# Gated linear recurrence feeding an ELU feed-forward block: the recurrence in 64-token chunks on four 64 by 64 array tiles, instead of 128-token chunks on two

## The chip, the cores and the metric

The kernel runs on one core of a Trainium2 chip. The metric is the device time of one execution in microseconds; lower is better. The engines are named as in the profile: PE is TensorE's matrix multiplication and PEld its loading of stationary weights, DVE is VectorE, ACT ScalarE, POOL GpSimd, SP the engine that issues most DMA transfers. L12 is line 12 of the kernel before.

## The reference

Two blocks follow each other. The first is a recurrence for each of 4 batches and 8 heads over 768 tokens, with a state of 48 by 48 and a gate for each of its rows:

```
f = sigmoid(f_logit)
for t in range(768):
    state = f[t][:, None] * state + outer(k[t], v[t])
    y[t]  = q[t] @ state
```

The second takes the outputs of all heads of a token side by side (3072 tokens by 384), multiplies by w_in (384 by 2048), applies ELU, which is h where h is positive and exp(h) − 1 elsewhere, and multiplies by w_out (2048 by 384). The inputs q, k, v and f_logit are float32; the weights come as 64-bit floats and are converted on the chip.

## The kernel before

`fast` (L356) does the work; `general` (L17) is a slower form for inputs outside its range, which a flag selects at the end. The tokens are cut into 12 units of 256 (U), three to a batch. Each unit has two chunks of 128 tokens (C). Heads lie in pairs: of each pair one head is on partitions 0 to 47 and the other on 64 to 111 (`HALF`); `FULL` names the two halves of 64 partitions.

For one unit, `gates` and `decays` (L522, L535) turn the gate into running products: ScalarE makes 1 + exp(−f) in place, VectorE scans it into g, takes the reciprocal p, and multiplies q by p, while POOL multiplies k by g. The scan starts anew at each chunk: POOL copies every C-th column into `restart` and sets it to zero in f. After that the recurrence inside a chunk is plain matrix work on TensorE, and between chunks one state is passed on:

- `transposed` (L562): k of one chunk, four head pairs, is transposed on TensorE into PSUM (psT) and copied by ScalarE to kn.
- `scores` (L570): for each head k times q of one chunk (psS, one PSUM bank for each half of the partitions), then VectorE multiplies by the causal mask into at.
- `advance` (L587): kn times v (psU); VectorE adds the state and multiplies by the chunk's decay, giving the next state. A batch's last chunk has no successor and skips this and its transpose.
- `outputs` (L608): v times at, and state times q, summed in psY; a batch's first chunk has no state and skips the second part. ScalarE copies psY to xt. After the second chunk, six DMA transfers issued by SP move the rows of the fourth head pair into the unused rows 48 to 63 and 112 to 127 of the first three (16 rows each, `PAD`), so that xt has three full blocks of 128 rows.

The feed-forward block goes in 16 steps per unit. `up` (L689) multiplies a block of w_in with xt (psH, 128 by 256, two buffers), ScalarE and VectorE apply ELU into gg; `down` (L705), two steps later (HLAG), multiplies gg with w_out and sums in psM.

The order of TensorE's work is written out by hand. In the main loop (L765 to L791), while unit m goes through the 16 steps of the feed-forward block, the attention of unit m + 1 is done in between: `attention` (L673) says behind which step each piece stands, and step s takes the pieces of entry s − 5. So before, steps 5 to 14 hold transposes, scores, update, scores, transposes, outputs, update, outputs. `prepare` (L553) issues one head pair's decays in each of the first steps. The start-up (L414 to L788, until `start.close()`) runs in the written order; later, a scheduler of the framework orders each engine's queue, and in the trace TensorE's order is the written one while VectorE does work of later units (decays, and the check of the weights' range at L504) early, as its inputs arrive. Unit 0 has a form of its own, `outputs_direct` (L638).

A product of float32 shows as two matmuls and two weight loads in the profile, a transpose as one. Where a matmul uses at most 64 rows or columns of the array, it occupies a tile of it: scores use two tiles of 64 rows by 128 columns, updates and the v part of outputs two of 128 by 64, the state part of outputs two of the four tiles of 64 by 64.

Of the kernel before, what the change touches and what calls it, by code (L numbers as in the profile page):

```python
# [8 lines left out]
FP32 = mybir.dt.float32  # L9
# [346 lines left out]
def fast(ctx: ExitStack, tc: tile.TileContext, q, k, v, f_logit, w_in, w_out, out, flag):  # L356
# [37 lines left out]
    vts, gts, pts, ats, kns, xts, sts = {}, {}, {}, {}, {}, {}, {}  # L394

    def load(u, other=None):

        b, s0 = u // UPB, (u % UPB) * U
        for n in "fkq":
            for r in range(2):  # L400
                ((other or nc.sync) if r else nc.sync).dma_start(
                    out=qkf[u % NB][n][HALF[r]],
                    in_=src[n][b, r::2, :, s0 : s0 + U].rearrange("p d s -> d p s"),
                )
        vts[u] = sb.tile([128, NCU, DM], FP32, tag="v", name=f"v{u}", bufs=3)
        nc.sync.dma_start(out=vts[u][:], in_=v[b, s0 : s0 + U].rearrange("(c t) n -> t c n", t=C))

    def blank(i, *engines):
# [13 lines left out]
    causal = cst.tile([128, C], FP32, name="causal")  # L422
# [3 lines left out]
        pattern=[[1, C]], channel_multiplier=-1,  # L426
    )
    for i in range(1, NB):
        blank(i, nc.gpsimd)
    fine = cst.tile([128, HP, NCU], FP32, name="fine")  # L430
    nc.vector.memset(fine[:], 1.0)
    py = ps.tile([128, HP, C], FP32, tag="y", name="psY")
# [89 lines left out]
    def gates(u, by_chunk=False):  # L522
# [4 lines left out]
        for i in range(2):  # L527
            a = f[:, :, i * C : (i + 1) * C] if by_chunk else f[:, 2 * i : 2 * i + 2]
            nc.scalar.activation(a, a, AF.Exp, scale=-1.0)
            nc.scalar.activation(a, a, AF.Copy, bias=1.0)  # L530
            if not by_chunk:
# [3 lines left out]
    def decays(u, pairs, cols):  # L535
        t = qkf[u % NB]
        g, p_ = gts[u], pts[u]
        for p in range(pairs.start, pairs.stop):
            a = t["f"][:, p, cols]
            nc.vector.tensor_tensor_scan(  # L540
                out=g[:, p, cols], data0=a, data1=a if cols.stop - cols.start == C else restart[:, p, cols],
# [20 lines left out]
    def transposed(u, c, bank="t"):  # L562

        pt = ps.tile([128, HP, 128], FP32, tag=bank, name=f"psT{u}_{c}")
        for p in range(HP):
            nc.tensor.transpose(pt[:, p, :], in_=qkf[u % NB]["k"][:, p, c * C : (c + 1) * C], identity=ident[:])  # L566
        kns[u, c] = sb.tile([128, HP, 128], FP32, tag="kn", name=f"kn{u}_{c}")
        nc.scalar.copy(kns[u, c][:], pt[:])  # L568

    def scores(u, c):  # L570
        t = qkf[u % NB]
        cols = slice(c * C, (c + 1) * C)
        at = ats[u, c] = sb.tile([128, 2, HP, C], FP32, tag="at", name=f"at{u}_{c}")
        pc = [ps.tile([128, HP, C], FP32, tag=f"s{r}", name=f"psS{u}_{c}_{r}") for r in range(2)]
# [6 lines left out]
        for r in range(2):  # L581
            nc.vector.tensor_tensor(  # L582
                out=at[:, r], in0=pc[r][:], in1=causal[:].unsqueeze(1).broadcast_to([128, HP, C]),
# [3 lines left out]
    def advance(u, c):  # L587

        if u % UPB == UPB - 1 and c == NCU - 1:
            return  # L590
        pu = ps.tile([128, HP, D], FP32, tag="t", name=f"psU{u}_{c}")
        for p in range(HP):
            for r in range(2):
                h = 2 * p + r
                nc.tensor.matmul(  # L595
                    pu[FULL[r], p], lhsT=kns[u, c][:, p, FULL[r]], rhs=vts[u][:, c, h * D : (h + 1) * D],
                    start=(p == 0), stop=(p == HP - 1), skip_group_check=True,
                )
        s = sb.tile([128, HP, D], FP32, tag="state", name=f"state{u}_{c}", bufs=3)
        now = pu[:]  # L600
        if u % UPB or c:
            nc.vector.tensor_tensor(out=s[:], in0=pu[:], in1=sts[u, c][:], op=ALU.add)
            now = s[:]
        decay = pts[u][:, :, (c + 1) * C - 1 : (c + 1) * C].broadcast_to([128, HP, D])
        nc.vector.tensor_tensor(out=s[:], in0=now, in1=decay, op=ALU.mult)
        sts[(u, c + 1) if c < NCU - 1 else (u + 1, 0)] = s

    def outputs(u, c):  # L608
        t = qkf[u % NB]
        cols = slice(c * C, (c + 1) * C)  # L610
        first = u % UPB == 0 and c == 0
        if c == 0:
            xts[u] = sb.tile([128, HP, U], FP32, tag="xt", name=f"xt{u}", bufs=3)
        at = ats.pop((u, c))
        for p in range(HP):
            for r in range(2):
                h = 2 * p + r
                nc.tensor.matmul(  # L618
                    py[HALF[r], p, :], lhsT=vts[u][:, c, h * D : (h + 1) * D], rhs=at[:, r, p],
                    start=(p == 0), stop=first, skip_group_check=True,  # L620
                )
        if not first:
            s = sts[u, c]
            for p in range(HP):
                for r in range(2):
                    nc.tensor.matmul(  # L626
                        py[HALF[r], p, :], lhsT=s[HALF[r], p], rhs=t["q"][HALF[r], p, cols],
                        start=False, stop=True, skip_group_check=True,
                    )
        nc.scalar.copy(xts[u][:, :, cols], py[:])  # L630
        if c == NCU - 1:
            x = xts[u]
            for i in range(2 * NKT):
                r, j = divmod(i, NKT)
                frm, g = 64 * r + j * PAD, 64 * r + D
                nc.sync.dma_start(out=x[g : g + PAD, j, :], in_=x[frm : frm + PAD, NKT, :])

    def outputs_direct(u, c):  # L638
# [5 lines left out]
        cols = slice(c * C, (c + 1) * C)  # L644
        q_ = qkf[u % NB]["q"]
        if c == 0:
# [190 lines left out]
```

## Time and profile before

| | |
|---|---|
| runs | 658.45, 1620.97 and 652.93 us; median 658.45 |
| the profiled execution | 655.96 us, of which the profile spans 654.2 |
| mean granted TensorE clock | 0.979 |
| TensorE busy from 61.5 to 611 us | all but 0.07 us |
| first psH matmul of unit 0 | 32.98 us |
| transfers of xt | 66 of 16 KB, 1.8 us from issue to landing |

A row of the timeline gives the start, the length, the engine, the line, the operation, the tiles it writes and reads with their shapes, how many instructions were merged, and in brackets how long the engine was idle before and what ended it. A row of the stretches gives the window, its length, and for each engine the busy time with the number of instructions, then the granted TensorE clock, the share of DMA time and GB/s. A row of the groups ends with the busy time, the mean duration in ns of one instruction, and the idle time before them with what ended most of it.

### The profile page before, as it was taken

The page shows a single profiled execution, that of the slowest core. Times are in us where ns is not written, and L with a number is a line of the kernel's source. Part 1 is how long each engine was busy: PE and PEld are TensorE (multiplying, and loading weights), DVE is VectorE, ACT ScalarE, POOL GpSimd, SP SyncE. Part 2 cuts the span into 40 slices and gives each one's busy share as a digit, 9 for nine tenths or more (in the row PEclk, how much of TensorE's full clock was granted, in tenths as well). Part 3 has the DMA queues.
Part 4 walks back from the last instruction along what each step waited for, and adds up shares of the span by engine and source line. Part 5 has one row for each costly group of instructions (what it writes and reads, how often), then busy time and mean ns, then how long its engine had stood idle before and what let it go on. Part 6 is the DMA issues. An engine that isn't in the chain of part 4 may idle for free.

```text
span 654.2 us, 8982 instructions
## 1 busy us (share of the span) xinstructions
PE 617.8 (94%) x3434; PEld 446.3 (68%) x3434; DVE 316.3 (48%) x527; ACT 228.3 (35%) x517; POOL 53.9 (8%) x110
## 2 busy tenths in 40 slices
PE   2765999999999999999999999999999999999995
PEld 2543777777777777777777777777777777777773
DVE  6779898895885236371237228271226221221110
ACT  2252444633534234323323233323333332323331
POOL 6011022220010010020010010010000000000000
PEclk9786999999999999999999999999999999999998
DMA  9999708686923013012012002011000000000000
GB/s 178 227 245 245 179 2 174 153 270 195 355 86 101 1 25 103 1 25 78 1 26 80 0 25 62 18 24 56 26 1 6 25 1 7 24 2 8 25 2 30
DMA packets 31926, 50.53 MB, mean 77 GB/s; under 512 B 3680, under 2 KB 24704, under 8 KB 31872
## 3 DMA queue, kind: packets, MB, share of 16 engines
q1 hardware_dynamic: 31248, 49.26, 29.0%
q10 hardware_dynamic: 624, 0.59, 0.4%
q8 instruction: 29, 0.48, 0.3%
q14 instruction: 25, 0.20, 0.1%
HBM read 44.04 MB, written 4.72 MB: 75 GB/s over the span
## 4 chain that ended last, share of the span: by engine, by line
PE 85%; DMA 8%; DVE 4%; issue 1%; POOL 0%; ACT 0%; DVEq 0%; SPq 0%; POOLq 0%
PE psH L693 37%; PE psM L711 36%; DMA raw<-in_moe_w_in_dram 6%; PE psS L577 4%; PE psY L618 3%; PE psY L626 3%; DMA q<-in_q_dram 2%; PE psU L595 2%; PE psT L566 1%; DVE p L544 1%; DVE g L540 1%; DVE spans L513 1%; DVE gg L701 0%; DVE q L546 0%; DVE at L582 0%
## 5 line engine op out<-in xcount | busy, mean ns | idle before, releaser
L693 PE MATMUL psH<-xt,wi 128*128 128x256 f32 x1152 | 290.0, 388 | 5.5 <-DVE gg L701 5.4
L711 PE MATMUL psM<-wo,gg 128*128 128x384 f32 x768 | 281.8, 490 | 0.0
L693 PEld LDWEIGHTS psH<-xt,wi 128*128 128x128 f32 x1152 | 213.4, 191 | 63.9 <-DVE gg L701 8.2
L701 DVE SCALAR_TENSOR_TENSOR gg<-e,psH 128x256 f32<-128x256 f32 x192 | 79.3, 413 | 281.9 <-ACT e L699 281.7
L711 PEld LDWEIGHTS psM<-wo,gg 128*128 128x128 f32 x768 | 147.4, 192 | 62.6 <-issue 1.7
L698 ACT ACTIVATE e<-psH 128x256 f32<-128x256 f32 x192 | 73.5, 383 | 300.3 <-PE psH L693 293.0
L544 DVE RECIPROCAL p<-g 128x256 f32<-128x256 f32 x48 | 83.0, 1740 | 0.6
L699 ACT ACTIVATE e<-e 128x256 f32<-128x256 f32 x192 | 79.8, 416 | 5.9
L546 POOL TENSOR_TENSOR k<-k,g 128x256 f32<-128x256 f32 x48 | 35.9, 768 | 262.2 <-DMA k<-in_k_dram 145.6
L582 DVE TENSOR_TENSOR at<-psS,causal 128x512 f32<-128x512 f32 x48 | 30.7, 682 | 18.6 <-PE psS L577 18.6
L577 PEld LDWEIGHTS psS<-q,k 48*128 48x128 f32 x384 | 24.2, 193 | 13.1 <-issue 12.1
L566 PE MATMUL psT<-ident,k 128*128 128x128 f32 x80 | 13.9, 293 | 19.2 <-POOL k L546 19.2
L513 DVE TENSOR_REDUCE spans<-again 128x1 f32<-128x768 f32 x32 | 29.3, 941 | 4.6 <-DMA again<-in_moe_w_in_dram 2.4
L630 ACT COPY xt<-psY 128x512 f32<-128x512 f32 x22 | 12.9, 586 | 49.8 <-PE psY L626 45.4
L540 DVE TENSOR_TENSOR_SCAN g<-f,restart 128x256 f32<-128x256 f32 x44 | 28.4, 693 | 1.6 <-POOL f L533 1.6
L577 PE MATMUL psS<-q,k 48*128 48x128 f32 x384 | 28.9, 291 | 0.0
L566 PEld LDWEIGHTS psT<-ident,k 128*128 128x128 f32 x80 | 10.5, 149 | 26.5 <-POOL k L546 20.1
L618 PEld LDWEIGHTS psY<-at,v 128*48 128x48 f32 x352 | 18.2, 122 | 12.0 <-issue 6.0
L618 PE MATMUL psY<-at,v 128*48 128x128 f32 x352 | 23.8, 277 | 0.0
L568 ACT COPY kn<-psT 128x512 f32<-128x512 f32 x20 | 11.7, 586 | 28.0 <-PE psT L566 28.0
L546 DVE TENSOR_TENSOR q<-q,p 128x256 f32<-128x256 f32 x48 | 20.4, 432 | 0.3
L626 PE MATMUL psY<-q,state 48*48 48x128 f32 x304 | 20.5, 274 | 0.0
(52 smaller groups left out, 193.5 us busy)
## 6 DMA issues: line engine op xcount, KB each, us to landing
raw<-in_moe_w_out_dram SPq DMA_DIRECT2D x8, 768.0 KB, 11.7
again<-in_moe_w_in_dram SPq DMA_DIRECT2D x8, 768.0 KB, 9.5
again<-in_moe_w_out_dram SPq DMA_DIRECT2D x8, 768.0 KB, 9.7
v<-in_v_dram SPq DMA_DIRECT2D x12, 384.0 KB, 5.0
raw<-in_moe_w_in_dram SPq DMA_DIRECT2D x16, 288.0 KB, 9.5
out_dram<-o SPq DMA_DIRECT2D x24, 192.0 KB, 1.9
f<-in_f_logit_dram SPq DMA_DIRECT2D x23, 192.0 KB, 7.6
k<-in_k_dram SPq DMA_DIRECT2D x23, 192.0 KB, 3.7
```

The source lines that it names most:

```text
L513: nc.vector.tensor_reduce(out=spans[:, i, n : n + 1], in_=raw[:].bitcast(FP32)[:, 1::2], axis=mybir.AxisListType.X, op=op, apply_absolute_ ...
L540: nc.vector.tensor_tensor_scan(out=g[:, p, cols], data0=a, data1=a if cols.stop - cols.start == C else restart[:, p, cols], initial=1.0, o ...
L544: nc.vector.reciprocal(p_[:, pairs, cols], g[:, pairs, cols])
L546: e.tensor_tensor(out=x[:, pairs, cols], in0=x[:, pairs, cols], in1=y[:, pairs, cols], op=ALU.mult)
L577: nc.tensor.matmul(pc[r][:, p], lhsT=t["k"][HALF[r], p, cols], rhs=t["q"][HALF[r], p, cols], start=True, stop=True,)
L618: nc.tensor.matmul(py[HALF[r], p, :], lhsT=vts[u][:, c, h * D : (h + 1) * D], rhs=at[:, r, p], start=(p == 0), stop=first, skip_group_chec ...
L626: nc.tensor.matmul(py[HALF[r], p, :], lhsT=s[HALF[r], p], rhs=t["q"][HALF[r], p, cols], start=False, stop=True, skip_group_check=True,)
L693: nc.tensor.matmul(ph[:], lhsT=wi[:, kt, s * 128 : (s + 1) * 128], rhs=xts[m][:, kt, :], start=(kt == 0), stop=(kt == NKT - 1),)
L698: nc.scalar.activation(e[:], ph[:], AF.Relu, scale=-1.0)
L699: nc.scalar.activation(e[:], e[:], AF.Exp, scale=-1.0)
L701: nc.vector.scalar_tensor_tensor(out=gs[T][:], in0=e[:], scalar=-1.0, in1=ph[:], op0=ALU.add, op1=ALU.max)
L711: nc.tensor.matmul(pms[m][i][:], lhsT=g[:, i * 128 : (i + 1) * 128], rhs=wo[:, s, :], start=(s == 0), stop=(s == NFT - 1),)
```

## The change

The chunk becomes 64 tokens (C = 64), so that a unit has four (NC); two chunks make a window of 128 (W, NW = 2). All four matrix products of the recurrence go over the four 64 by 64 tiles of the array, chosen by the head's half (r) and the chunk's parity (b). The even chunk of a window lies on the lower 64 token rows, the odd one on the upper. A unit's attention is in four entries instead of eight (the change counts nine blocks): both transposes at step 5, scores and state updates together at step 7, the v part of the outputs at step 9, the state part at step 12. Scores are masked by `twice`, which holds the 64 by 64 causal mask on both halves of the partitions. The two transposes use the PSUM banks t and y, and so do the two sums of the update; the output sums use the banks s0 and s1 of the scores.

In the outputs, the product of an odd chunk writes to the half of the other head (`r ^ b`), so its heads come out swapped, and the copies to xt swap them back: one copy for the even chunks and two of 64 partitions for the odd ones. The stationary v of a head is 64 columns wide there instead of 48, so v's tiles get 16 more columns, set to zero at the start, and are three fixed buffers instead of a pool's. The update is computed for every chunk, the last of a batch too, and its state is left out there; four states a unit are added and decayed on VectorE (three in a batch's last unit). Unit 0 keeps 128-token chunks, and `restart` is filled at 4 columns a pair instead of 2. POOL fills `twice` and clears the padding of v in the start-up, ahead of its clearing of the second and third input buffers.

```diff
-    C = 128
+    C = 64
+    W = 2 * C
     U = 256
-    NCU = U // C
+    NW = U // W
+    NC = U // C
...
+    vs = [cst.tile([128, NW, DM + PAD], FP32, name=f"v{i}") for i in range(NB)]
...
-        nc.sync.dma_start(out=vts[u][:], in_=v[b, s0 : s0 + U].rearrange("(c t) n -> t c n", t=C))
+        nc.sync.dma_start(
+            out=vs[u % NB][:, :, 0:DM], in_=v[b, s0 : s0 + U].rearrange("(c t) n -> t c n", t=W)
+        )
...
+    twice = cst.tile([128, C], FP32, name="twice")
+    for b in range(2):
+        nc.gpsimd.tensor_copy(twice[FULL[b]], causal[FULL[b], FULL[b]])
+    for i in range(NB):
+        nc.gpsimd.memset(vs[i][:, :, DM:], 0.0)
...
+    def stepped(u, c, pu, end):
+
+        s = sb.tile([128, HP, D], FP32, tag="state", name=f"state{u}_{c}", bufs=6)
+        now = pu
+        if u % UPB or c:
+            nc.vector.tensor_tensor(out=s[:], in0=pu, in1=sts[u, c][:], op=ALU.add)
+            now = s[:]
+        decay = pts[u][:, :, end - 1 : end].broadcast_to([128, HP, D])
+        nc.vector.tensor_tensor(out=s[:], in0=now, in1=decay, op=ALU.mult)
+        sts[(u, c + 1) if end < U else (u + 1, 0)] = s
+
+    def scores(u):
+
...
+        pc = [ps.tile([128, NW, HP, C], FP32, tag=f"s{r}", name=f"psS{u}_{r}") for r in range(2)]
+        for w in range(NW):
+            for p in range(HP):
+                for b in range(2):
+                    cols = slice(w * W + b * C, w * W + b * C + C)
+                    for r in range(2):
+                        nc.tensor.matmul(
+                            pc[r][FULL[b], w, p], lhsT=t["k"][HALF[r], p, cols], rhs=t["q"][HALF[r], p, cols],
+                            start=True, stop=True,
+                        )
+        for r in range(2):
+            nc.vector.tensor_tensor(
+                out=at[:, r].rearrange("k w p i -> k (w p) i"), in0=pc[r][:].rearrange("k w p i -> k (w p) i"),
+                in1=twice[:].unsqueeze(1).broadcast_to([128, NW * HP, C]), op=ALU.mult,
+            )
+
+    def advance(u):
+
+        last = u % UPB == UPB - 1
+        pu = [ps.tile([128, NW, HP, D], FP32, tag=n, name=f"psU{u}_{n}") for n in ("t", "y")]
+        for w in range(NW):
+            for p in range(HP):
+                for r in range(2):
+                    h = 2 * p + r
+                    for b in range(2):
+                        nc.tensor.matmul(
+                            pu[b][FULL[r], w, p], lhsT=kns[u, w][FULL[b], p, FULL[r]],
+                            rhs=vs[u % NB][FULL[b], w, h * D : (h + 1) * D],
+                            start=(w == 0 and p == 0), stop=(w == NW - 1 and p == HP - 1), skip_group_check=True,
+                        )
+        for c in range(NC - last):
+            stepped(u, c, pu[c % 2][:, c // 2], (c + 1) * C)
+
+    def outputs(u):
...
+        pys[u] = [ps.tile([128, NW, HP, C], FP32, tag=f"s{b}", name=f"psY{u}_{b}") for b in range(2)]
...
+                for r in range(2):
+                    h = 2 * p + r
+                    for b in range(2):
+                        nc.tensor.matmul(
+                            pys[u][b][FULL[r ^ b], w, p], lhsT=vs[u % NB][FULL[b], w, h * D : h * D + 64],
+                            rhs=at[FULL[b], r, w, p], start=(w == 0 and p == 0), stop=False,
+                            skip_group_check=True,
+                        )
+
+    def carried(u):
...
+                for b in range(2):
+                    c = 2 * w + b
+                    if (u % UPB, c) == (0, 0):
+                        continue
+                    for r in range(2):
+                        nc.tensor.matmul(
+                            py[b][HALF[r ^ b], w, p], lhsT=sts[u, c][HALF[r], p],
+                            rhs=t["q"][HALF[r], p, c * C : (c + 1) * C],
+                            start=False, stop=True, skip_group_check=True,
+                        )
+        x = xts[u] = sb.tile([128, HP, U], FP32, tag="xt", name=f"xt{u}", bufs=3)
+        to = x[:].rearrange("n p (w b i) -> n b w p i", b=2, i=C)
+        nc.scalar.copy(to[:, 0], py[0][:])
+        for r in range(2):
+            nc.scalar.copy(to[FULL[r], 1], py[1][FULL[1 - r]])
...
     def attention(u):
 
-        last = u % UPB == UPB - 1
         return {
-            0: [lambda: transposed(u, 0)],
-            1: [lambda: scores(u, 0)],
-            3: [lambda: advance(u, 0)],
-            4: [lambda: scores(u, 1)],
-            5: [] if last else [lambda: transposed(u, 1)],
-            6: [lambda: outputs(u, 0)],
-            8: [lambda: advance(u, 1)],
-            9: [lambda: outputs(u, 1)],
+            0: [lambda: transposed(u, 0, "t"), lambda: transposed(u, 1, "y")],
+            2: [lambda: scores(u), lambda: advance(u)],
+            4: [lambda: outputs(u)],
+            7: [lambda: carried(u)],
         }
```

More of the change, by code (lines that the diff above doesn't have):

```diff
@@ L420, in fast @@
     make_identity(nc, ident)
[L422 removed]
+    causal = cst.tile([128, W], FP32, name="causal")
     nc.gpsimd.memset(causal[:], 1.0)
@@ L560, in prepare, with transposed @@
         watch(u)
[L562 to L564 removed]
+    def transposed(u, w, bank):
+        pt = ps.tile([128, HP, 128], FP32, tag=bank, name=f"psT{u}_{w}")
         for p in range(HP):
[L566 to L568 removed]
@@ L570, in scores @@
-    def scores(u, c):
-        t = qkf[u % NB]
-        cols = slice(c * C, (c + 1) * C)
-        at = ats[u, c] = sb.tile([128, 2, HP, C], FP32, tag="at", name=f"at{u}_{c}")
-        pc = [ps.tile([128, HP, C], FP32, tag=f"s{r}", name=f"psS{u}_{c}_{r}") for r in range(2)]
+            nc.tensor.transpose(pt[:, p, :], in_=qkf[u % NB]["k"][:, p, w * W : (w + 1) * W], identity=ident[:])
+        kns[u, w] = sb.tile([128, HP, 128], FP32, tag="kn", name=f"kn{u}_{w}")
+        nc.scalar.copy(kns[u, w][:], pt[:])
@@ L604, in advance @@
[L604 to L636, printed above, removed]
```

102 lines of the change are left out of this document (56 added, 46 removed).

## The prediction, made before the changed kernel ran

> **What bounds the kernel now.** First the page, for span and busy shares, and the share of the chain that ended last by engine; then that chain in order of time; then busy time by stretch.
>
> ```profile
> span 654.2 us, 8982 instructions
> PE 617.8 (94%) x3434; PEld 446.3 (68%) x3434; DVE 316.3 (48%) x527; ACT 228.3 (35%) x517; POOL 53.9 (8%) x110
> PE 85%; DMA 8%; DVE 4%; issue 1%; POOL 0%; ACT 0%; DVEq 0%; SPq 0%; POOLq 0%
> ...
> 47.10 9.32 DMA raw<-in_moe_w_in_dram
> 61.50 2.56 PE psH L693 x6
> ...
> 125.49 3.18 DVE p L544 x2
> ...
> 151.32 1.56 PE psH L693 x6
> ```
> ```profile
> 61.50:112.00 50.50, 50.50 (x284) 35.92 (x284) 44.63 (x69) 24.84 (x51) 6.31 (x14) 0.95 0.56 124
> 112.00:161.00 49.00, 48.93 (x274) 35.40 (x273) 41.76 (x66) 23.02 (x52) 11.19 (x26) 1.00 0.73 201
> 161.00:211.00 50.00, 50.00 (x282) 36.23 (x281) 35.67 (x56) 21.97 (x51) 3.64 (x8) 1.00 0.61 193
> 562.00:611.00 49.00, 49.00 (x275) 35.40 (x274) 10.18 (x23) 15.36 (x37) 0.00 (x0) 1.00 0.03 11
> ```
> Up to 61.5 us weights arriving by DMA set the pace. From there TensorE never rests: 50.50 of 50.50 us, 48.93 of 49.00, and so on to the end, while VectorE falls from 44.6 to 10.2. Only from 125 to 151 does the chain run over VectorE, and there TensorE has no slack to give either. So any TensorE time removed after 61.5 us comes off the span, except where VectorE is nearly as full (the first two stretches).
>
> Next the TensorE timeline of one unit, which gives each attention block's price in this stream. The column after the start is modelled length; I use starts.
>
> ```profile
> 463.65 1.45 PE L711 MATMUL psM<-wo,gg 128*128 128x384 f32 x4
> 464.94 0.60 PE L566 MATMUL psT<-ident,k 128*128 128x128 f32 x4
> 465.38 1.46 PE L693 MATMUL psH<-xt,wi 128*128 128x256 f32 x6
> 466.68 1.45 PE L711 MATMUL psM<-wo,gg 128*128 128x384 f32 x4
> 468.06 1.16 PE L577 MATMUL psS<-q,k 48*128 48x128 f32 x16
> 469.15 1.56 PE L693 MATMUL psH<-xt,wi 128*128 128x256 f32 x6
> 470.55 1.45 PE L711 MATMUL psM<-wo,gg 128*128 128x384 f32 x4
> 471.84 1.46 PE L693 MATMUL psH<-xt,wi 128*128 128x256 f32 x6
> 473.13 1.45 PE L711 MATMUL psM<-wo,gg 128*128 128x384 f32 x4
> 474.52 0.67 PE L595 MATMUL psU<-v,kn 128*64 128x48 f32 x16
> 475.12 1.56 PE L693 MATMUL psH<-xt,wi 128*128 128x256 f32 x6
> 476.52 1.45 PE L711 MATMUL psM<-wo,gg 128*128 128x384 f32 x4
> ...
> 493.18 1.45 PE L711 MATMUL psM<-wo,gg 128*128 128x384 f32 x4
> 494.56 1.08 PE L618 MATMUL psY<-at,v 128*48 128x128 f32 x16
> 495.57 1.08 PE L626 MATMUL psY<-q,state 48*48 48x128 f32 x16
> 496.58 1.56 PE L693 MATMUL psH<-xt,wi 128*128 128x256 f32 x6
> 497.98 1.45 PE L711 MATMUL psM<-wo,gg 128*128 128x384 f32 x4
> ...
> 501.86 1.46 PE L693 MATMUL psH<-xt,wi 128*128 128x256 f32 x6
> ```
> An undisturbed step is 2.58 us (470.55 to 473.13). A block's price is the distance between the psM groups around it less 2.58: transposes 466.68−463.65−2.58 = 0.45; scores 3.87−2.58 = 1.29; state update 3.39−2.58 = 0.81; both output parts 4.80−2.58 = 2.22, of which the state part is 1.01 (495.57 to 496.58).
>
> **What one small matmul costs.** Each call shows as two matmuls. Four transposes, 128 moving columns each on the whole array, take 0.44 us: 110 ns each. Sixteen psY matmuls with as many columns take 1.01: 63 each. So two tiles do run side by side, eight slots of 110 ns plus about 0.33 for entering and leaving the tiled form (1.21 for the first output part). The psU block is 0.41 us shorter than psY (1.01 against 0.60 to the next start), so its slot is 110−51 = 59 ns. Its 48 moving columns would take 48×110/128 = 41, its 64 weight columns 55, so I read 59 as the weight load.
>
> ```profile
> 12.97 2.12 PE L577 MATMUL psS<-q,k 48*128 48x128 f32 x16
> 15.02 1.09 PE L595 MATMUL psU<-v,kn 128*64 128x48 f32 x16
> ```
> In the start-up, with the array slow, psS is stretched from 1.16 to 2.12 and psU from 0.67 to 1.09: psU follows the array too, so 59 is array work and not a fixed price per instruction.
>
> **The change part by part.** Before, a middle unit costs 2 transposes 0.90 + 2 scores 2.58 + 2 updates 1.62 + 2 outputs 4.44 = 9.54 us. A batch's last unit skips one transpose and one update (8.28), its first one state part (8.53). After 61.5 us run units 1 to 11: four middle, four last, three first.
>
> After: 8 transposes 0.90. Scores and updates are 64 matmuls each (twice as many, half the columns or half the rows) and stand together, both 64 by 64: 128 matmuls. Outputs are 64, state parts 64 (48 in a first unit, whose first chunk has no state: there two tiles idle for half of the block, and the slots stay 16). All load 64 or 48 weight columns and stream 64 or 48. No row shows four tiles at once. From below: two column tiles read the same rows at once (psU, psY) and two row tiles fill the same columns at once (psS), so four in a slot, 59/4 = 14.8 ns each. From above: the densest row, two in 59, 29.5 each. I take the lower end, since each pairing that four need has a row. Then scores with updates are 32 slots, 1.89+0.36 = 2.25; outputs 16 slots, 0.94+0.33 = 1.27; state part 1.27. Sum 5.69. Gain: 4×3.85 + 4×2.59 + 3×2.84 = **34.3 us**.
>
> The Trainium skill, "TensorE: Matmul & The Clock Gate", section "Measured speedup vs the span model", gives four row tiles 3.07 times the speed of one, not 4. An estimate by that figure makes a matmul 59/3.07 = 19.2 ns and the gain 12 us smaller; the psY row (63 of a possible 55) shows a milder loss of this kind for two.
>
> VectorE: scores need two multiplies of 682 ns where four stood, four state steps have eight operations of 356 where two had four.
>
> ```profile
> L582 DVE TENSOR_TENSOR at<-psS,causal 128x512 f32<-128x512 f32 x48 | 30.7, 682 | 18.6 <-PE psS L577 18.6
> L602 DVE TENSOR_TENSOR state<-psU,state 128x192 f32<-128x192 f32 x16 | 5.7, 356 | 9.0 <-PE psU L595 9.0
> L630 ACT COPY xt<-psY 128x512 f32<-128x512 f32 x22 | 12.9, 586 | 49.8 <-PE psY L626 45.4
> 496.70 0.59 ACT L630 COPY xt<-psY 128x512 f32<-128x512 f32 x1 [2.48 <-PE psY L626]
> 497.31 3.69 SPq L636 DMA_DIRECT2D xt<-xt  x6
> ```
> That is −1.36+1.42 us, nothing; but now 1.36+2.85 = 4.2 us stand together ahead of one step's gg, which TensorE wants only two steps (5.2 us) later, so it is hidden wherever VectorE is idle half the time. The outputs wait for the masked scores two steps after them instead of five; that wait is covered by gg's own, which stands behind those multiplies and is due in the same step. The state chain has five steps (12.9 us) for 2.85 us. Its cover is thin only where VectorE is nearly full: up to 151 us. There the before chain already ran over VectorE for 26 us with nothing to spare, and unit 1 and 2 would bring 3.85+2.59 = 6.4 us. I take **2 us lost** there (0 to 6.4).
>
> ScalarE copies xt in three pieces of 0.586, one more, and twice the transposed keys also in last units; at 35% busy nothing waits for that. The six SP transfers of xt are as before. The last copy comes at step 12 instead of 14, so it and its transfers (issued 497.31 to 501.00, due 501.86) gain 5.2−1.2 us of room. The second transpose moves to step 5 and waits for the same keys as the first. Queues and loads are unchanged after the start.
>
> Start-up: POOL gets two copies and three small memsets ahead of its blanking. If the memset of the padding waits for the first v transfer, POOL's later blanks shift.
>
> ```profile
> 2.99 0.44 SPq L406 DMA_DIRECT2D v<-in_v_dram  x1
> ...
> 8.57 0.96 POOL L520 MEMSET restart<- 128x1024 f32 x1
> ...
> 9.49 0.73 POOL L546 TENSOR_TENSOR k<-k,g 128x256 f32<-128x256 f32 x1
> ```
> Between nothing and about 5 us at 9.49; I take nothing, because weights set 61.5 us.
>
> **Sum.** 654.2 − 34.3 + 2 = 621.9 us of span. The profiled execution took 655.96, 1.8 more than its span, and lies midway between the two near runs (652.93, 658.45), so no further shift: **624 us**; its own range 616 to 632.
>
> **The rivals.**
>
> *One matmul per 29.5 ns*, because four tiles do not run together or because matmuls are handed out no faster. Then 256 matmuls take 7.55 us and a unit 9.47 with transposes and entries, a first one (240 matmuls) 9.00: middle −0.07, last +1.19, first +0.47, together +5.9 us; 660 of span, 662 in all, slower than before. It decides from about 27 ns per matmul (34.3/(11×252) = 12.4 above 14.8). For it: no row is denser. Against: psU scales with the array. The Trainium skill, "TensorEngine Tiling (Array Packing)", section "Instruction Overhead", speaks for it: some 60 cycles per matmul, however few its columns; at the 2.4 GHz that it gives the array this is an estimate of 25 ns and a time near 652, and no row here shows a tile with fewer than 48 columns. Chance 0.14, and 0.04 for something still dearer (loads not hidden behind streaming).
>
> *Partial overlap*, three of four tiles at work: 256×59/3 = 5.03 against 3.78, +1.25 in eight units and +0.94 in the three first: 637. Speaking for it, each call is two matmuls on one tile in a row, so the fourth tile's work stands six places behind; against it, psS and psY pair up in spite of that. Chance 0.10.
>
> *VectorE takes over* in the first three units (44.6, 41.8, 35.7 busy of 50): their gain of 3.85+2.59+2.84 is lost instead of 2: 631. For it the chain from 125 to 151; against it that its work there is partly taken ahead of need. Chance 0.10.
>
> Forecast: 0.62.
>
> **How the numbers follow.** 2% is about what a measurement of this kernel can tell from no change: faster means below 643. Faster holds the forecast, VectorE and partial overlap, 0.82; I keep 0.78, since a milder floor between 15 and 29.5 ns lies between cases. Within 2% 0.17, slower 0.05. The range runs from 616 (59 ns shrinking to the 55 of its columns, 64×4 ns×11 = 2.8; no loss, 2; and 3 for the distance between runs) to 648 (three of four tiles, with POOL's 5 us and the rest of VectorE's 6.4 on top), leaving 0.18 out above.
>
> **What would show it.** Right: about 4,920 matmuls instead of 3,434; each 64-matmul block spans about 1 us and the double one 2; TensorE still without gaps from 61 us on; the step at each block 2.58 plus 2.25, 1.27, 1.27. Wrong: blocks of 1.9 and 3.8 us (two tiles or a floor), gaps at psH released by gg before 160 us (VectorE), or psT late at 10 us with all of the start behind it.

## The result, and the profile after

The changed kernel takes **628.34 us** (median of 4 runs, 627.95 to 628.63) against 658.58 for the kernel before on the same chip: a ratio of 0.957, 95% interval 0.951 to 0.963. One of the four executions of before took 1620.97 us; the ratio compares the mean of the other three (656.69) with that of after (628.32), so it is not the quotient of the two medians. The forecast was 624 us. The profiled execution took 628.63 us. Line numbers from here on are those of the changed kernel: psH is L749, psM L767, gg L757.

The page of after first: span, engines, and the chain that ended last by engine.

```profile
span 626.8 us, 12052 instructions
PE 584.9 (93%) x4922; PEld 428.7 (68%) x4922; DVE 316.6 (51%) x549; ACT 235.7 (38%) x532; POOL 55.3 (9%) x115
PE 77%; DVE 10%; DMA 8%; issue 2%; ACT 1%; POOL 1%; DVEq 0%; SPq 0%; POOLq 0%; ACTq 0%
```

The matmuls number 4922, where some 4,920 were forecast. VectorE's work is as it was (316.6 against 316.3), but its share of the chain went from 4% to 10%.

Next TensorE's timeline, one unit late in the run. The column after the start is modelled length; prices are distances between starts.

```profile
421.81 1.45 PE L767 MATMUL psM<-wo,gg 128*128 128x384 f32 x4
...
425.64 1.45 PE L767 MATMUL psM<-wo,gg 128*128 128x384 f32 x4
...
446.32 1.45 PE L767 MATMUL psM<-wo,gg 128*128 128x384 f32 x4
...
449.78 1.45 PE L767 MATMUL psM<-wo,gg 128*128 128x384 f32 x4
...
452.36 1.45 PE L767 MATMUL psM<-wo,gg 128*128 128x384 f32 x4
...
455.06 0.22 PE L621 MATMUL psU_t<-v,kn 64*64 64x48 f32 x1
455.07 0.22 PE L621 MATMUL psU_y<-v,kn 64*64 64x48 f32 x1
455.08 0.22 PE L621 MATMUL psU_t<-v,kn 64*64 64x48 f32 x1
455.08 0.22 PE L621 MATMUL psU_y<-v,kn 64*64 64x48 f32 x1
455.12 0.22 PE L621 MATMUL psU_t<-v,kn 64*64 64x48 f32 x1
...
457.16 1.45 PE L767 MATMUL psM<-wo,gg 128*128 128x384 f32 x4
459.74 1.45 PE L767 MATMUL psM<-wo,gg 128*128 128x384 f32 x4
...
463.62 1.45 PE L767 MATMUL psM<-wo,gg 128*128 128x384 f32 x4
```

Four matmuls of the updates start within 0.02 us, and the next four 0.06 us later: all four tiles work in one slot (the time from one such start to the next). Between the two psM of each pair, and by the same subtraction of 2.58 us as in the prediction, lie the state part (from 421.81: 1.25), the transposes (from 446.32: 0.88), scores and updates (from 452.36: 2.22) and the v part (from 459.74: 1.30), 5.65 us a unit; forecast were 5.69.

So the new blocks gain what they should. Where it was not kept shows in TensorE's timeline at the first psH of unit 1 and at the end, before and then after; a bracket is idle time and what ended it.

```profile
101.29 0.59 PE L693 MATMUL psH<-xt,wi 128*128 128x256 f32 x2
...
642.70 4.03 PE L711 MATMUL psM<-wo,gg 128*128 128x384 f32 x12
```
```profile
94.23 1.13 PE L749 MATMUL psH<-xt,wi 128*128 128x256 f32 x4 [1.88 <-DVE gg L757]
...
99.94 0.92 PE L749 MATMUL psH<-xt,wi 128*128 128x256 f32 x3 [0.27 <-DVE gg L757]
...
134.08 1.13 PE L749 MATMUL psH<-xt,wi 128*128 128x256 f32 x4 [1.05 <-DVE gg L757]
...
144.48 1.56 PE L749 MATMUL psH<-xt,wi 128*128 128x256 f32 x6 [1.15 <-DVE gg L757]
...
148.00 1.35 PE L749 MATMUL psH<-xt,wi 128*128 128x256 f32 x5 [0.67 <-DVE gg L757]
...
434.68 0.59 PE L749 MATMUL psH<-xt,wi 128*128 128x256 f32 x2
...
481.69 0.59 PE L749 MATMUL psH<-xt,wi 128*128 128x256 f32 x2
...
616.67 3.39 PE L767 MATMUL psM<-wo,gg 128*128 128x384 f32 x10
```

Pass m is the 16 feed-forward steps of unit m, with the attention of unit m + 1 in it. A late pass takes 47.0 us (434.68 to 481.69), without a gap. But in the first passes psH waits for gg, which it did not before. From the first psH of unit 1 to the end of the last psM, before takes 642.70 + 4.03 − 101.29 = 545.4 us and after 616.67 + 3.39 − 99.94 = 520.1: 25.3 us less. By the measured blocks units 2 to 11 should have gained 30.9 (the prediction's sum with 5.65, or 5.63 in a first unit: 3 × 3.89 + 4 × 2.63 + 3 × 2.90). **Some 5.6 us are lost behind 99.94, and more in pass 0.**

What stands ahead of those late gg is in VectorE's timeline of after, the first two stretches in pass 0, the others in pass 1.

```profile
68.77 0.42 DVE L757 SCALAR_TENSOR_TENSOR gg<-e,psH 128x256 f32<-128x256 f32 x1 [0.49 <-ACT e L755]
70.30 1.29 DVE L607 TENSOR_TENSOR at<-psS,twice 128x512 f32<-128x512 f32 x2 [1.11 <-PE psS L602]
71.51 0.35 DVE L586 TENSOR_TENSOR state<-psU_t,state 128x192 f32<-128x192 f32 x1
...
74.31 0.36 DVE L589 TENSOR_TENSOR state<-state,p 128x192 f32<-128x192 f32 x1
...
77.05 0.41 DVE L757 SCALAR_TENSOR_TENSOR gg<-e,psH 128x256 f32<-128x256 f32 x1
...
90.99 1.27 DVE L551 TENSOR_TENSOR_SCAN g<-f,restart 128x256 f32<-128x256 f32 x2
92.17 1.73 DVE L555 RECIPROCAL p<-g 128x256 f32<-128x256 f32 x1
93.82 0.36 DVE L757 SCALAR_TENSOR_TENSOR gg<-e,psH 128x256 f32<-128x256 f32 x1
...
128.12 3.36 DVE L555 RECIPROCAL p<-g 128x256 f32<-128x256 f32 x2
...
132.00 1.75 DVE L555 RECIPROCAL p<-g 128x256 f32<-128x256 f32 x1
133.66 0.36 DVE L757 SCALAR_TENSOR_TENSOR gg<-e,psH 128x256 f32<-128x256 f32 x1
...
139.72 4.38 DVE L524 TENSOR_REDUCE spans<-again 128x1 f32<-128x768 f32 x5
144.03 0.40 DVE L757 SCALAR_TENSOR_TENSOR gg<-e,psH 128x256 f32<-128x256 f32 x1
...
145.22 2.42 DVE L551 TENSOR_TENSOR_SCAN g<-f,restart 128x256 f32<-128x256 f32 x4
147.57 0.38 DVE L757 SCALAR_TENSOR_TENSOR gg<-e,psH 128x256 f32<-128x256 f32 x1
```

The gg of 93.82, 133.66, 144.03 and 147.57 end the gaps at 94.23, 134.08, 144.48 and 148.00. Right ahead of them stand two kinds of work: reciprocals and scans (decays), and in pass 1 the reductions of the range check of the weights (`spans`). A third is the double masking with all four state steps in a lump, in pass 0 from 70.3 to 74.6 us. No gap follows it at once; but behind it VectorE still converts weights and gives out a gg only every 2.79 us (77.05, 79.84, 82.62, 85.41, 88.20), more than the 2.58 of a step, so that it does not catch up before unit 2's decays come at 90.99. A unit has four scans and four reciprocals, in the order of the units; counted off, the reciprocals from 125 to 134 are unit 4's, whose attention is in pass 3, and the scans from 145 are unit 6's, of pass 5. Three causes were therefore tried.

### The profile page after: what moved, and what is told of

The parts are those of the page before. It is cut to its first block, busy times and chain, and to the rows that moved or that the text cites. A ratio compares the mean times of both kernels' runs of the same rounds, so it can differ in the third digit from the quotient of the medians.

```text
span 626.8 us, 12052 instructions
## 1 busy us (share of the span) xinstructions
PE 584.9 (93%) x4922; PEld 428.7 (68%) x4922; DVE 316.6 (51%) x549; ACT 235.7 (38%) x532; POOL 55.3 (9%) x115
## 3 DMA queue, kind: packets, MB, share of 16 engines
q1 hardware_dynamic: 31248, 49.26, 29.5%
## 4 chain that ended last, share of the span: by engine, by line
PE 77%; DVE 10%; DMA 8%; issue 2%; ACT 1%; POOL 1%; DVEq 0%; SPq 0%; POOLq 0%; ACTq 0%
PE psH L749 35%; PE psM L767 34%; DMA raw<-in_moe_w_in_dram 4%; DVE p L555 3%; DMA q<-in_q_dram 2%; DVE g L551 2%; DVE spans L524 2%; PE psS L602 2%; PE psY L639 2%; PE psT L577 2%; DMA f<-in_f_logit_dram 1%; PE psY L656 1%; DVE gg L757 1%; PE psU_t L621 1%; DVE bits L500 1%
## 5 line engine op out<-in xcount | busy, mean ns | idle before, releaser
L749 PE MATMUL psH<-xt,wi 128*128 128x256 f32 x1152 | 287.4, 386 | 11.3 <-DVE gg L757 11.2
L767 PE MATMUL psM<-wo,gg 128*128 128x384 f32 x768 | 281.7, 490 | 0.0
L749 PEld LDWEIGHTS psH<-xt,wi 128*128 128x128 f32 x1152 | 215.3, 191 | 76.7 <-DVE gg L757 19.9
L757 DVE SCALAR_TENSOR_TENSOR gg<-e,psH 128x256 f32<-128x256 f32 x192 | 79.0, 412 | 273.7 <-ACT e L755 273.6
L767 PEld LDWEIGHTS psM<-wo,gg 128*128 128x128 f32 x768 | 147.6, 192 | 62.6 <-issue 1.8
L577 PE MATMUL psT<-ident,k 128*128 128x128 f32 x96 | 14.8, 295 | 19.6 <-POOL k L557 19.6
L577 PEld LDWEIGHTS psT<-ident,k 128*128 128x128 f32 x96 | 12.1, 152 | 24.7 <-POOL k L557 20.5
L607 DVE TENSOR_TENSOR at<-psS,twice 128x512 f32<-128x512 f32 x22 | 14.1, 685 | 10.0 <-PE psS L602 10.0
L479 ACT ACTIVATE raw<-raw 128x768 int32<-128x768 uint32 x16 | 14.3, 911 | 7.7 <-DMA raw<-in_moe_w_out_dram 6.1
L540 ACT ACTIVATE f<-f 128x512 f32<-128x512 f32 x24 | 14.2, 621 | 6.3 <-DMA f<-in_f_logit_dram 5.7
L500 DVE CUSTOM_DVE_ANT_0 bits<-raw,bits 128x1536 uint16<-128x1536 uint16 x16 | 15.3, 959 | 2.4 <-ACT raw L479 1.6
L543 POOL COPY restart<-f 128x8 f32<-128x8 f32 x22 | 7.3, 332 | 101.2 <-ACT f L541 69.8
L639 PEld LDWEIGHTS psY<-at,v 64*64 64x64 f32 x704 | 11.3, 135 | 6.0 <-issue 2.7
L602 PEld LDWEIGHTS psS<-q,k 48*64 48x64 f32 x704 | 11.3, 134 | 6.0 <-issue 6.0
```

The costliest lines, as they stand in the source:

```text
L602: nc.tensor.matmul(pc[r][FULL[b], w, p], lhsT=t["k"][HALF[r], p, cols], rhs=t["q"][HALF[r], p, cols], start=True, stop=True,)
L639: nc.tensor.matmul(pys[u][b][FULL[r ^ b], w, p], lhsT=vs[u % NB][FULL[b], w, h * D : h * D + 64], rhs=at[FULL[b], r, w, p], start=(w == 0 ...
L749: nc.tensor.matmul(ph[:], lhsT=wi[:, kt, s * 128 : (s + 1) * 128], rhs=xts[m][:, kt, :], start=(kt == 0), stop=(kt == NKT - 1),)
L757: nc.vector.scalar_tensor_tensor(out=gs[T][:], in0=e[:], scalar=-1.0, in1=ph[:], op0=ALU.add, op1=ALU.max)
L767: nc.tensor.matmul(pms[m][i][:], lhsT=g[:, i * 128 : (i + 1) * 128], rhs=wo[:, s, :], start=(s == 0), stop=(s == NFT - 1),)
```

## The experiments

All are edits of the changed kernel. The last column is the time from the first psH of unit 1 to the end of the last psM in the profiled execution. It leaves the start out: the first psH of unit 1 came anywhere from 96.7 to 103.0 us in these executions, so that the whole times of one kernel scatter by up to 6 us. From there on, a pass in which TensorE waits for nothing repeats closely: pass 4 takes 46.97 us in after, 1, 2, 5, 6 and 9. Runs 1 to 4, 5 to 7 and 8 and 9 were taken on three chips, on which before took 657.84, 654.89 and 655.81 us (medians), so between them the ratios compare better than the times.

| kernel | us, median (range) | to before, 95% interval | from unit 1 to the end |
|---|---|---|---|
| after | 628.34 (627.95–628.63) | 0.957 (0.951–0.963) | 520.1 |
| 1 without range checks | 627.27 (626.06–628.94) | 0.955 (0.951–0.959) | 519.0 |
| 2 range checks later | 626.62 (624.07–628.38) | 0.954 (0.949–0.958) | 519.1 |
| 3 two tiles at a time | 652.74 (652.15–653.34) | 0.994 (0.987–1.000) | 544.5 |
| 4 update in its own entry | 626.22 (625.52–629.36) | 0.954 (0.950–0.959) | 520.7 |
| 5 state steps later | 628.34 (626.96–630.16) | 0.959 (0.956–0.961) | 521.0 |
| 6 = 2 and 5 | 626.84 (623.47–628.65) | 0.956 (0.954–0.959) | 518.9 |
| 7 runs of eight | 642.12 (one run) | | 533.4 |
| 8 decays held | 621.84 (620.82–626.50) | 0.949 (0.946–0.951) | 515.8 |
| 9 = 2, 5 and 8 | **619.03** (618.08–621.68) | 0.946 (0.943–0.949) | 514.5 |

### 1 and 2: the range checks, left out or tied to their pass

In the first the checks are gone; in the second a small copy from xt of the asking pass stands ahead of each check's transfer, so that it can't run early.

```diff
...
-                check(4 * (m - 4) + s - NFT + 4)
+                pass
...
-        if wide:
+        if False:
...
```


> Changed kernel without the 32 range checks of the weights on VectorE (spans), their eight-odd transfers and their part of the flag: the check that the weights lie in range is left out. Theory A (the 7 us between forecast and result are lost because VectorE is full up to 196 us, with range checks standing ahead of gg in its queue): the waits of psH for gg after 100 us, 4.4 us in units 2 to 5, fall below 1 us, and the profiled execution goes from 628.6 to about 624.5. The 2.2 us lost in unit 1 (before 100 us, where weights are converted) stay. Theory B (they are lost because masks and four state steps, 4.2 us in a row, stand ahead of one gg): waits and time stay, 628 within 1.

```diff
...
+        nc.scalar.copy(raw[:].bitcast(FP32)[:, 0:1], xts[m][:, 0, 0:1])
         nc.sync.dma_start(out=raw[:], in_=flat[n // 2])
...
```


> Changed kernel with each range check tied to its place in the written order: before a check's transfer ScalarE writes one column of the buffer from that unit's xt, so that the transfer and the two reductions cannot run before it. All work is done, 16 short ScalarE copies are added. Theory A: as without checks, about 624.5 to 625, the reductions standing after 240 us, where VectorE is idle half of the time. Theory B: 628 within 1. A third outcome, over 629, if the late checks meet the steps with masks and states and make gg late there.

Both miss what the checks alone would have given: about 1 us comes off (519.0 and 519.1 instead of 520.1), and pass 1 keeps 2.5 us of gaps in either (1.04 and 1.43), where after has 2.9. The reductions were in the way, but other work takes their place ahead of gg: in 1 the second of these gaps, at 141.0 us, stands behind the four scans of unit 6.

### 3 and 7: does the order of the tiles matter

In 3 each product does all its even chunks, then all its odd ones, so neighbours in the order share two tiles. In 7 the two pairs of tiles change every eight matmuls (sixteen instructions). Of the four products, the cuts show the loops of the scores.

```diff
-        for w in range(NW):
-            for p in range(HP):
-                for b in range(2):
+        for b in range(2):
+            for w in range(NW):
+                for p in range(HP):
...
```


> Changed kernel with the chunk's parity as the outermost loop in the four products, so that 32 matmuls in a row go to only two of the four tiles. Same matmuls, same number, same shapes. If the price is one slot of 59 ns for as many tiles as are at work (the forecast's reading): a block of 64 takes 32 slots, 1.9 instead of 0.95 us, a unit 3.8 more (3.3 in a first), 40 us in all, of which up to 6 hide in the waits for VectorE: 662 to 669. If a matmul costs a fixed 15 ns whatever its tile: 628 within 1. If TensorE looks further ahead than 16 matmuls and fills the idle tiles from later in its queue: in between, 630 to 655.


```diff
         for w in range(NW):
-            for p in range(HP):
-                for b in range(2):
+            for b in range(2):
+                for p in range(HP):
...
```


> The same matmuls as after, in runs of eight (16 instructions) on two of the four tiles, then eight on the other two, four runs to a block. If PE starts matmuls of other tiles past the ones that queue on a busy tile, as the longer runs (16 matmuls on two tiles, two runs to a block) let it seem, with about 5 slots of 59 ns won at each change: three changes to a block win 15 of the 16 slots that could be won, steady unit 46.97 + 0 to 0.4 us. If only neighbours in the order overlap: two tiles at a time, 46.97 + 3.8 = 50.7 us.

The timelines of 3 and of 7, each first psH of unit 8 and of unit 9:

```profile
401.13 0.59 PE L749 MATMUL psH<-xt,wi 128*128 128x256 f32 x2
...
451.04 0.38 PE L749 MATMUL psH<-xt,wi 128*128 128x256 f32 x1
```
```profile
395.92 0.59 PE L751 MATMUL psH<-xt,wi 128*128 128x256 f32 x2
...
444.43 0.38 PE L751 MATMUL psH<-xt,wi 128*128 128x256 f32 x1
...
464.67 0.25 PE L622 MATMUL psU_t<-v,kn 64*64 64x48 f32 x1
464.71 0.22 PE L602 MATMUL psS<-q,k 48*64 48x64 f32 x2
464.76 0.22 PE L622 MATMUL psU_t<-v,kn 64*64 64x48 f32 x1
464.77 0.23 PE L602 MATMUL psS<-q,k 48*64 48x64 f32 x2
464.82 0.22 PE L622 MATMUL psU_t<-v,kn 64*64 64x48 f32 x1
464.83 0.23 PE L602 MATMUL psS<-q,k 48*64 48x64 f32 x2
464.88 0.45 PE L622 MATMUL psU_t<-v,kn 64*64 64x48 f32 x10
```

A unit takes 49.91 us in 3 and 48.51 in 7, against 46.97, and 3 in all 652.74, which is the third of its outcomes (630 to 655). Strictly two tiles at a time would add 64 slots of 59 ns, 3.78 us; 3 adds 2.94, and 7 adds 1.54. The rows of 7 show why: at a change of tiles the first psU start while psS that stand ahead of them are still being handed out, for three slots (464.71, 464.77, 464.83), and then two tiles work alone again. In 3 there are five changes a unit and 0.84 us won, 2.8 slots each; in 7 thirteen and 2.24 us, 2.9 slots each. The expectation for 7 reckoned with 5 slots, a misreading of 3; with 2.8 it would have been 48.6. So both outcomes that it named are refuted, and most of the gain of four tiles rests on the order in which the code hands the tiles out. The whole time of 7 is from a single run; the prices of its units are from the trace, at a granted clock of 1.00.

### 4: the update in an entry of its own

```diff
-            2: [lambda: scores(u), lambda: advance(u)],
+            2: [lambda: scores(u)],
+            3: [lambda: advance(u)],
```


> Changed kernel with the state update one step after the scores instead of right behind them, so five entries into the tiled form instead of four per unit. If entering and leaving costs 0.33 to 0.36 us (the forecast's term): 11 times 0.35, +3.8 us, less what hides in waits for VectorE: 631 to 632.5. Theory B (the lump on VectorE is what costs): the lump is split, the waits for gg after 100 us shrink by half or more, which gives back 2 to 3 us: 629 or less. Theory A: waits for gg stay near 4 us.

A late unit takes 47.33 us instead of 46.97: the extra entry into the tiled form costs 0.36 us, as the prediction read it. Ten such entries lie behind the first psH of unit 1, 3.6 us, and 3.0 of them are won back in passes 1 to 3, where the gaps shrink; pass 0 gains 1.4 from step 5 on, its entry paid. The time of 626.22 is under the 631 to 632.5 that the entry alone would give and within theory B's 629 or less, and the gaps behind 100 us fell by half, from 4.1 to 2.1 us, as B had it: that seemed to speak for the lump of maskings and state steps as the cause. But from unit 1 on 4 takes 520.7 us, no less than after; the lower time comes from pass 0 and the start.

### 5 and 6: the state steps later, alone and with the later checks

The same split of the lump, without the extra entry.

```diff
         for c in range(NC - last):
+            yield
             stepped(u, c, pu[c % 2][:, c // 2], (c + 1) * C)
...
-            2: [lambda: scores(u), lambda: advance(u)],
+            2: [lambda: scores(u), step],
+            3: [step, step],
             4: [lambda: outputs(u)],
+            5: [step, step],
```


> The matmuls of the update stay in entry 2; the four state steps of a unit (add and multiply on VectorE) are given out two at entry 3 and two at entry 5, so that VectorE no longer has two maskings and eight state operations ahead of one gg. No entry is added. Theory B (the lump on VectorE holds up psH): the stalls of the pass of unit 0 behind the double block go, the ones of passes 1 and 2 shrink as they did when the update had an entry to itself, and the price of that entry (0.36 us x 11 = 4.0 us) is not paid: 626.2 - 4.0 = 622 us (621 to 624), 516 to 518 us from the first psH of unit 1 to the end instead of 520.1. Theory A (only the range checks that run ahead hold it up): 628 us as after, 520 us from that psH to the end. Steady unit 46.97 us by both, since nothing stalls there.

> The state steps given out at entries 3 and 5, and the transfers of the range check tied to the pass that asks for them. If the two causes add up (each took about 1 to 2 us of passes 1 to 5 by itself): 1 us under the kernel with the state steps alone, 620 to 622 us, 515 to 517 us from the first psH of unit 1 to the end, stalls of psH on gg in passes 1 to 5 under 1.5 us in sum. If the lump is all of it: equal to the kernel with the state steps alone within 0.5 us. If VectorE is simply full in passes 0 and 1, whatever the order: 625 us or more, stalls of 2 us or more left in pass 1.

In 5, pass 0 from step 5 on loses 1.3 us of stalls (37.0 us instead of 38.3), and there a gg stands between maskings and states. From the psH of step 7, the first behind the scores and updates, to the first psH of unit 1 it is 28.84 us in each of after, 1 and 2, where the lump is whole, and 27.56, 27.59 and 27.59 in 5, 6 and 9, where it is split: 1.3 us in six traces. But pass 1 keeps its gaps (1.04, 1.14 and 0.67 against 1.05, 1.15 and 0.67), and the time from unit 1 on is 521.0: theory B's 621 to 624 us fail. The 628.34 are what theory A named, of which 1 and 2 had left about 1 us. In pass 1 the scheduler put the state steps straight behind the maskings again, so that there the experiment did not do what it was meant to; whether the lump matters in pass 1 it leaves open (9 answers that). With the checks later too (6) it is 518.9, and pass 1 still has 2.5 us of gaps; that is the third outcome named for 6, VectorE simply full whatever the order, which 8 refutes.

### 8: decays held to the pass before their own

Two small copies from xt of unit m into f of unit m + 2 stand ahead of its transfer, so that unit m + 2's decays can't start before pass m.

```diff
             if s == (8 if m == 0 else 0) and m + 2 < NU:
+                for r in range(2):
+                    nc.scalar.copy(qkf[(m + 2) % NB]["f"][HALF[r], 0, 0:1], xts[m][HALF[r], 0, 0:1])
                 load(m + 2)
```


> The changed kernel, with one edit: two small copies on ScalarE from xt of unit m into f of unit m + 2 stand ahead of its transfer, so that the decays of unit m + 2 can't be taken on VectorE before pass m has begun. In the trace after, the decays of units 3 and 4 and the scans of 5 and 6 all fall into pass 1, where only unit 2's are due. Theory C (the stalls of passes 1 to 3 come from work of later units that the schedule puts ahead of gg): from the first psH of unit 1 to the end 514.2 us is what it takes without a stall (ten passes of 46.97, one of 44.21, 0.3 more); after takes 520.1; with the decays held 515 to 517, some 622 to 625 us in all. Rival, capacity (VectorE has more to do in passes 0 to 2 than fits, and what is held back only stalls later): 519 us or more, 627 to 628 us in all. Rival, lateness (held decays come too late for the transposes): gaps at psT in every pass, 522 us or more.

TensorE's timeline of 8, and below it one stretch of it (columns as in the stretches of before):

```profile
102.95 0.59 PE L749 MATMUL psH<-xt,wi 128*128 128x256 f32 x2
...
614.70 4.03 PE L767 MATMUL psM<-wo,gg 128*128 128x384 f32 x12
```
```profile
112.00:161.00 49.00, 49.00 (x433) 36.34 (x432) 39.21 (x64) 19.51 (x47) 4.63 (x10) 1.00 0.86 277
```
The same stretch of after:
```profile
112.00:161.00 49.00, 46.14 (x418) 33.35 (x417) 43.54 (x69) 24.44 (x55) 10.54 (x26) 1.00 0.73 217
```

515.8 us from unit 1 on, 621.84 in all, as the decays' theory had it and neither rival: TensorE is busy 49.00 us of 49.00, and passes 1 to 3, which took 146.8 us in after, take 140.9, three times 46.97. VectorE still does 39.2 us of work in that stretch (43.5 in after), the range checks above all with 17.3, and holds nobody up; the decays that left it found room in later passes. So the amount was not too much, only its place in the queue. Holding has a price too: the held decays now stand in the first steps of a pass, and passes 4, 6 and 7 are 0.3, 0.95 and 0.3 us longer than 46.97, 1.6 us in sum. (The profiled execution took 626.5 us: it reached unit 1 only at 102.95, and its granted clock was 0.50 from 97.4 to 100.8 us.)

### 9: all three

The edits of 2, 5 and 8 together.

> The three edits together: state steps at entries 3 and 5, transfers of the range check tied to the pass that asks for them, decays held to the pass before their own. If the stalls are a matter of what stands ahead of gg, and not of how much VectorE has to do: 514.2 to 515.5 us from the first psH of unit 1 to the end, stalls in pass 0 as with the state steps alone, 620 to 623 us in all. If VectorE's amount of work in passes 0 to 2 is the limit: 518 us or more, 625 us or more.

```profile
96.69 0.81 PE L755 MATMUL psH<-xt,wi 128*128 128x256 f32 x3
...
607.78 3.39 PE L773 MATMUL psM<-wo,gg 128*128 128x384 f32 x10
```
514.5 us from unit 1 on and **619.03** in all (0.946, interval 0.943 to 0.949), a little under the 620 to 623 expected. That is 9.3 us under the time of after, but before, too, took less there (655.81 against 658.58); by the ratios to before, 0.946 against 0.957, it is some 7 us, of which 5.6 lie behind the first psH of unit 1. Against before, the stretch from unit 1 to the end is now 545.4 − 514.5 = 30.9 us shorter, which is what the measured blocks of units 2 to 11 come to. The price of holding is nearly gone: passes 4 and 7 take 46.97 us and pass 6 47.11. In pass 0 one gap of 1.43 us is left, at 91 us, behind unit 2's decays; holding these back as well was not tried. In pass 1 of this kernel the lump is still whole, two maskings and six state operations from 117.2 to 120.8 us without a gg between them, and no gap follows: there, by itself, it is hidden, as the prediction had it.

## Why the prediction was right, and where not

- **The prices of the blocks held.** Four tiles share a slot of 59 ns, 14.8 ns a matmul: chosen from two pairings seen apart, and shown by the rows at 455. In the trace of after, psU, with 48 moving columns, and psS, with 64, both start four matmuls every 58 ns; both have 64 weight columns. So the slot does not follow the moving columns there, which fits the prediction's reading of 59 as the weight load. Forecast 5.69 a unit, measured 5.65; the entry's 0.33 to 0.36 us was measured alone as 0.36 (experiment 4). The rivals of one matmul per 29.5 ns and of three tiles out of four are out: the double block would have cost 4.1 us or 2.9, and cost 2.22. Experiment 3 shows what two tiles, as far as the order holds TensorE to them, would have made of the change: 0.994 of before, next to nothing. The Trainium skill's figure of 3.07 for four row tiles ("TensorE: Matmul & The Clock Gate", section "Measured speedup vs the span model") and its 60 cycles per matmul ("TensorEngine Tiling (Array Packing)", section "Instruction Overhead") spoke for dearer blocks, the latter if each matmul adds its 60 cycles whatever its tile; with four starts within 0.02 us and 64 in under a microsecond, no run here bears that out for tiles of 64 by 64. The "milder loss" that the prediction saw in the psY row (63 of a possible 55) is none either: inside that block of before a pair of matmuls starts every 109 to 110 ns, 55 for each, and the rest of the 1.01 us is spent at the block's beginning and end.
- **Step hidden at no cost, rightly:** the start-up (first psH of unit 0 at 32.88 us after, 32.98 before), the copies on ScalarE, the transfers of xt (psH waits for none of them).
- **The term that was mis-sized is "I take 2 us lost there (0 to 6.4)".** Blocks give 34.8 us, the span fell by 654.2 − 626.8 = 27.4: 7.4 were lost, beyond the upper bound too. With 7 in its place the sum comes to 627 of span, 629 in all, still inside the forecast's own range of 616 to 632. (The upper end of 648 does not follow from its terms: 637, 5 and the remaining 4.4 make 646.) The stretch was named rightly as the one where VectorE is nearly full, but the loss ran on to 241 us, where the last gap is, and it was argued from the wrong mechanism. The prediction looked at the lump of maskings and state steps ahead of one gg; that costs 1.3 us in pass 0 (experiments 5, 6 and 9), and nothing in pass 1 once the other work is out of the way (experiment 9). The main part, the 5.9 us that passes 1 to 3 lasted over late ones, went altogether when the decays alone were held (experiment 8).
- **The rival "VectorE takes over" had its evidence turned round.** That VectorE's work "is partly taken ahead of need" was put down as speaking against it. It is the main cause: decays that no pass before the third or fifth needs stand in VectorE's queue ahead of the gg that TensorE waits for next. Before the change the same early work was there (its reciprocals from 125 to 134 us as well), and the chain of waits ran over it from 125 to 151; that the longer attention blocks then just covered it was not tried by itself. But experiments 3 and 7, made for another purpose, bear it out: with the same work on VectorE and longer units, passes 1 to 3 exceed passes 4 to 6, whose units are of the same kinds, by less. From the psH of step 2 on it is 5.7 us in after (units of 46.97 us), 4.7 in 7 (48.51) and 2.2 in 3 (49.91); before, with 49.6 to 50.9 us a unit, it is 0.5.
- **"TensorE still without gaps from 61 us on" was wrong,** and the sign that the prediction gave for it, gaps at psH released by gg before 160 us, is what came.

The waits of psH on gg, before and after (total us, times, longest), say it in a line each. Two waits of each kernel lie in the start (5.4 us before, 5.0 after); behind 61 us before has none, and after seven of 6.2 us in sum.
```profile
PE psH L693 <- DVE gg L701: 5.4, 2, 3.0
```
```profile
PE psH L749 <- DVE gg L757: 11.2, 9, 2.6
```

Open remain the share of unit 2's decays in pass 0 (the gap of 1.43 us that 9 still has), and how much of experiment 4's smaller gaps in passes 1 to 3 came from the longer units and how much from another order; the scheduler orders VectorE's queue anew for each kernel, and no run holds that order fixed.

## What to carry to other kernels

When the bounding engine gets faster by a few per cent, look at each engine whose queue it waits on not for its busy share but for what stands in that queue ahead of the next result needed; work prefetched several stages early costs nothing only as long as the stage is long enough to cover it, and a chain of waits that already runs over such an engine without a gap is the warning. Work can be held back by tying its input transfer to a result of the stage before, which here was worth more than splitting or removing work. Small matmuls on separate array tiles run together if the order hands out the tiles in turn; here runs of sixteen matmuls on one pair of tiles lost 2.94 of the 3.78 us a unit that four tiles win over two, and runs of eight 1.54.

## What the runs showed of the hardware that was not expected

TensorE starts matmuls out of program order across array tiles, but only a short way: at a change of tiles 2.8 to 2.9 slots of two matmuls were won in both experiments 3 and 7, and psU started ahead of six psS that stand before it in the written order (that the queue holds that order is read from the rest of the trace, not from these rows). The Trainium skill, "TensorE: Matmul & The Clock Gate", section "The mechanism", says that matmuls start and end in program order; the rows of experiment 7 at 464.67 and 464.71 differ from that, and here the measurement decides. The state part, with 48 weight columns and 64 moving ones, costs 1.25 us where the v part, with 64 and 64, costs 1.30. In the trace of after the slots are 56 ns in the state part and 58 in the v part, so a slot is not the same for all, and both lie near what 64 columns take (55 ns by the prediction's 110 for 128).
